# Weight conversion shared by ScalarE and VectorE, views for V's parts, and a scheduler that counts the port of VectorE and GpSimd

## The chip, the cores and the metric

One core of a Trainium2 chip runs one launch. The metric is the device time of that launch in microseconds (us), the median over runs. PE is TensorE's matmul stream and PEld its weight loads, DVE is VectorE, ACT ScalarE, POOL GpSimd, SP the queue that issues all DMAs.

## What is computed

Attention for 4 batches of 8 heads, sequence 576, head size 64, with scores below (row maximum - tau) cut off, then two gated layers of 512 x 1536:

```
scores = (q @ k.T) / 8
attn   = exp(where(scores >= max - tau, scores, -1e9) - max) / sum
x      = (attn @ v), heads side by side          # 2304 tokens x 512
xn     = x / sqrt(mean(x*x) + 1e-6) * rms_g
y      = (silu(xn @ w_gate) * (xn @ w_val)) @ w_out
out    = (silu(y @ w2_gate) * (y @ w2_val)) @ w2_out
```

The inputs q, k, v are float32. The six weight matrices arrive as float64, and the kernel makes them float32 on the chip.

## The kernel before

**Work units.** A batch of attention is 36 tiles of 128 queries (9 for each pair of heads, `tile_ops`). The two layers of a batch are 36 units (18 each): a unit is one slice of weights, 128 x 1024 elements, and 48 matmuls of 128x128 by 128x288. Every value that goes into a dense matmul stands there as two float32r parts, x0 = rounded x and x1 = x - x0, and three of the four products are taken (`dense`). A layer's `gate_val` unit makes one 128-row slice of the hidden values: tanh on ACT (L647), two products on DVE (L648, L659), a cast on ACT (L663) and the rest x - x0 on POOL or DVE (L666). `outp` units multiply those slices with the output weights and add up Y on DVE (L694).

**A tile** goes through QK on PE (L386), the negative row maximum on DVE (L409), the threshold and bias on DVE (L410, two elements), exp on ACT (L411), mask and sum on DVE (L412), small DVE operations and a reciprocal (L418 to L424), the normalisation (`normalise`, on ACT, DVE or POOL by a table), and a split into two float16 parts (`parts16`: a high part by a cast, L344 to L348; a low part in two subtractions, L352 and L353). DMA transposes (L358) bring the parts to PE, which multiplies them with V (`pv`, L444 and L447). `split` prepares V: two bfloat16 copies of the upper part (L304 or L306) and two subtractions (L311 or L313) for each head.

**Weights** (`weights(n)`, one call for each of the 36 units): load of 1 MB of float64 (L571), then five operations on the words: an absolute value of the upper word on ACT (L576), and on DVE a clamp (L579), a shift (L580) and two shift-and-or steps (L581, L582). Then a cast to float32r on ACT (L583), the rest on POOL (L584), and a store of both parts, 1 MB, to device memory (L585). Batches 1 to 3 load these stored parts (L565). The raw words have 2 buffers (`w64`), the float32 words 3 (`w32`), the split parts 3 (`w`).

**Order.** Nothing is ordered by hand. Each operation is put on record with an engine, a cost in ns, a priority and its dependences (`Program.op`). `Program.order` is a list scheduler: it always takes the engine that is free first and starts its ready operation of smallest priority, and the instructions are then issued in the order of the start times so found. Priorities are a due time, `SU(n)` for unit n and `ST(n)` for tile n, plus an offset from the tables `OFF` and, for the 36 tiles of batch 0, `OFFF`.

The attention of batch 0 runs alone. The dense units of batch 0 run beside the attention of batch 1 and the conversion of all weights, those of batches 1 and 2 beside the attention of batches 2 and 3, those of batch 3 alone.

Of the kernel before, what the change touches and what calls it, by code (L numbers as in the profile page):

```python
# [20 lines left out]
U64 = mybir.dt.uint64  # L21

# [52 lines left out]
class Program:  # L75


    def __init__(self):
        self.eng, self.cost, self.deps, self.fn, self.prio, self.lat, self.name, self.cols, self.rel = [], [], [], [], [], [], [], [], []
        self.wrote, self.read = {}, {}  # L80

    def op(self, eng, cost, fn, r=(), w=(), bufs=(), p=0.0, lat=None, name='', cols=None, rel=0.0):
# [21 lines left out]
        self.rel.append(rel)  # L104
        self.name.append(name)
# [3 lines left out]
    def order(self):  # L109
# [19 lines left out]
        out, seen = [], {}  # L129
        while len(out) < n:  # L130
# [10 lines left out]
            _, i = heapq.heappop(go[e])  # L141
            start[i] = t
# [36 lines left out]
def body(ctx: ExitStack, tc: tile.TileContext, qkv, tau, w1, rg, w2, outT):  # L179
# [19 lines left out]
    OFFF.update({'REC': -1394, 'PVO': 2852, 'THR': 2066, 'SQA': 9944, 'DT': -5666, 'PV': 13886, 'MAX': 1101, 'EXP': -137, 'MASK': 1731, 'LO': 3517, 'HI': -1687, 'SQ': -13503, 'NORM': 4425, 'LOL': -41192})
# [35 lines left out]
    r_raw = ring("raw", 4, [P, NQ], F32)  # L235
    r_v12 = ring("v12", 3, [P, 5, P], BF16)
# [12 lines left out]
    r_w64 = ring("w64", 2, [P, 1024], U64)  # L249
    r_w32 = ring("w32", 3, [P, 1024], F32)  # L250
# [551 lines left out]
```

## Time and profile before

| | |
|---|---|
| three runs | 1333.31, 1334.6, 1335.15 us, median 1334.6 |
| profiled execution | 1335.63 us, span 1333.8 us |
| busy over the span | PE 91%, PEld 80%, DVE 62%, ACT 44%, POOL 41% |
| granted TensorE clock, mean | 0.951 |
| DMA | 261.48 MB, mean 196 GB/s |

The profile shows one execution. Its span runs from the first to the last instruction; the execution's own time is 1.8 us longer. A share over the whole span mixes stages that differ, so it is read by stages. These are cut here at the first tanh of each batch's dense units (170, 527, 820 and 1105 us) and at the end of the last exp of batch 0 (125 us).

### The profile page before, as it was taken

Reading aid. Unit: us, or ns where it says so; the run is one execution under the profiler, and the core shown is the slowest. Engines: PE = TensorE matmul, PEld = TensorE weight load, DVE = VectorE, ACT = ScalarE, POOL = GpSimd, SP = SyncE. Lnnn points to the kernel's source line nnn. Section 1 sums busy time; section 2 is a strip of 40 time slices with the busy share of each in tenths; the row PEclk is TensorE's granted clock in tenths of the full one; section 3 lists DMA queues with packets and bytes.
Section 4 is the critical chain, followed back from the end, with each engine's and each line's share of the span. In section 5 each row is a group of like instructions: output and inputs, shape, how many; then the busy total and the mean of one; then the engine's idle time right before and its main releaser. Section 6 shows DMA issues by size and latency. Waiting matters only on the chain.

```text
span 1333.8 us, 21809 instructions
## 1 busy us (share of the span) xinstructions
PE 1211.9 (91%) x8528; PEld 1068.6 (80%) x8528; DVE 833.2 (62%) x1636; ACT 586.7 (44%) x878; POOL 545.7 (41%) x507
## 2 busy tenths in 40 slices
PE   4666669888889879999999999999999999999998
PEld 2334458777778778888888888888889899999998
DVE  6999798999999996545545565445554442122122
ACT  4555356645666544544444444544444321212111
POOL 4678566756666645323342423323431221012010
PEclk9767579999999889999999999999999999999999
DMA  7778748786888887976666658676556545454443
GB/s 219 158 183 195 216 140 251 218 253 188 255 245 238 243 271 205 286 211 186 186 188 185 181 161 229 186 192 195 175 164 170 164 169 181 164 177 166 158 168 122
DMA packets 204807, 261.48 MB, mean 196 GB/s; under 512 B 175008, under 2 KB 175648, under 8 KB 181664
## 3 DMA queue, kind: packets, MB, share of 16 engines
q1 hardware_dynamic: 204704, 260.08, 66.2%
q8 instruction: 67, 1.10, 0.3%
q14 instruction: 36, 0.29, 0.1%
HBM read 175.11 MB, written 42.47 MB: 163 GB/s over the span
## 4 chain that ended last, share of the span: by engine, by line
PE 63%; DVE 27%; issue 4%; ACT 3%; DMA 2%; POOL 1%; SPq 0%; DVEq 0%; ACTq 0%; POOLq 0%
PE ps L609 54%; PE ps L386 4%; DVE w L581 3%; DVE w L582 3%; PE pt L444 3%; DVE e L412 2%; DVE e L352 2%; DVE col L409 2%; DVE w L579 2%; DVE col L410 2%; PE pt L447 1%; DVE w L580 1%; DVE th L659 1%; DVE th L648 1%; DVE e L353 1%
## 5 line engine op out<-in xcount | busy, mean ns | idle before, releaser
L609 PE MATMUL ps<-XS,w 128*128 128x288 f32 x4608 | 661.7, 302 | 15.4 <-DVE th L648 4.4
L609 PEld LDWEIGHTS ps<-XS,w 128*128 128x128 f32 x4608 | 630.9, 192 | 55.2 <-issue 33.5
L609 PE MATMUL ps<-h,w 128*128 128x288 f32 x2304 | 322.1, 297 | 0.0
L609 PEld LDWEIGHTS ps<-h,w 128*128 128x128 f32 x2304 | 308.4, 189 | 17.1 <-issue 16.3
L666 POOL TENSOR_TENSOR h<-th,h 128x576 fp32r<-128x576 f32 x72 | 110.7, 1537 | 395.0 <-ACT h L663 386.6
L386 PE MATMUL ps<-raw 64*128 64x288 f32 (+1 forms) x640 | 121.7, 501 | 75.4 <-DVE e L412 49.9
L648 DVE SCALAR_TENSOR_TENSOR th<-th,ps 128x576 f32<-128x576 f32 x94 | 70.7, 752 | 184.2 <-ACT th L647 183.9
L411 ACT ACTIVATE e<-ps,col 128x576 f32<-128x576 f32 x126 | 93.3, 741 | 170.3 <-DVE col L410 164.4
L663 ACT CAST h<-th 128x576 fp32r<-128x576 f32 x96 | 64.7, 674 | 176.2 <-DVE th L659 175.9
L386 PEld LDWEIGHTS ps<-raw 64*128 64x128 f32 (+1 forms) x640 | 47.7, 195 | 113.4 <-DVE e L412 60.6
L409 DVE TENSOR_REDUCE col<-ps 128x1 f32<-128x576 f32 x144 | 107.7, 750 | 46.0 <-PE ps L386 45.3
L412 DVE SCALAR_TENSOR_TENSOR e<-ps,col,e 128x576 f32<-128x576 f32 x126 | 102.4, 813 | 48.1 <-ACT e L411 47.8
L333 ACT ACTIVATE e<-e,col 128x576 f32<-128x576 f32 x100 | 86.8, 868 | 81.0 <-DVE col L424 81.0
L584 POOL TENSOR_TENSOR w<-w,w 128x1024 fp32r<-128x1024 f32 x36 | 88.8, 2467 | 68.7 <-ACT w L583 63.7
L659 DVE SCALAR_TENSOR_TENSOR th<-th,ps 128x576 f32<-128x576 f32 x94 | 70.6, 751 | 68.8 <-PE ps L609 68.7
L444 PE MATMUL pt<-ag,v 128*128 128x256 f16 (+1 forms) x576 | 93.0, 313 | 19.7 <-DMA ag<-e 18.7
L647 ACT ACTIVATE th<-ps 128x576 f32<-128x576 f32 x94 | 61.1, 650 | 108.8 <-PE ps L609 108.1
L444 PEld LDWEIGHTS <-v 128*128 128x128 bf16 x576 | 55.7, 106 | 48.5 <-issue 14.2
L344 ACT CAST e<-e 128x576 f16<-128x576 f32 x122 | 81.7, 670 | 17.3 <-POOL e L329 13.3
L694 DVE TENSOR_TENSOR Y<-ps,Y 128x576 f32<-128x576 f32 x64 | 48.3, 755 | 64.0 <-PE ps L609 63.7
L352 POOL TENSOR_TENSOR e<-e,e 128x512 f16<-128x512 f32 x68 | 87.6, 1288 | 0.0
L353 POOL TENSOR_TENSOR e<-e,e 128x64 f16<-128x64 f32 x68 | 24.7, 364 | 105.6 <-ACT e L344 104.9
(89 smaller groups left out, 1061.8 us busy)
## 6 DMA issues: line engine op xcount, KB each, us to landing
w<-kept SPq DMA_DIRECT2D x108, 1024.0 KB, 4.9
w<-in_w SPq DMA_DIRECT2D x36, 1024.0 KB, 6.5
kept<-w SPq DMA_DIRECT2D x36, 1024.0 KB, 5.4
raw<-in_qkv SPq DMA_DIRECT2D x31, 736.0 KB, 5.2
out<-Y SPq DMA_DIRECT2D x16, 288.0 KB, 3.5
ag<-e SPq DMA_TRANSPOSE x160, 3.2
raw<-in_qkv SPq DMA_DIRECT2D x2, 160.0 KB, 2.8
raw<-in_qkv SPq DMA_DIRECT2D x1, 224.0 KB, 3.3
```

The source lines that it names most:

```text
L333: op("ACT", 765, lambda: nc.scalar.activation(e, e, AF.Identity, bias=c[:, 4:5], scale=c[:, 3:4]), **k)
L352: op(en, 610 if eng == 2 else 1113, lambda: n1.tensor_tensor(h[:, 640:], e[:, :512], h[:, :512], ALU.subtract), w=[("lo", n)], p=T + F['LO ...
L386: nc.tensor.matmul(s[m:m + w, j, :HS], x[k, c0:c0 + w], x[k, S + j * HS:S + (j + 1) * HS], start=True, stop=True)
L409: op("DVE", 668, lambda: nc.vector.tensor_reduce(c[:, 0:1], s2, AX.XY, ALU.max, negate=True), w=[sk, ("mx", n)], bufs=[cb], p=T + F['MAX'] ...
L411: op("ACT", 625, lambda: nc.scalar.activation(e2, s2, AF.Exp, bias=c[:, 2:3], scale=SCALE), r=[("thr", n)], w=[sk, ("e", n)] + ek, bufs=[c ...
L412: op("DVE", 730, lambda: nc.vector.scalar_tensor_tensor(e2, s2, c[:, 1:2], e2, ALU.is_ge, ALU.mult, accum_out=c[:, 6:7]), r=[("thr", n)], ...
L444: nc.tensor.matmul(pv_[:, :w], v12.t[:, i if i < 5 else i - 5, :], o[:, i, :w], start=(i == 0), stop=False)
L584: op("POOL", 2300, lambda: nc.gpsimd.tensor_tensor(ws[:, 1], w, f32(ws[:, 0]), ALU.subtract), r=[("w32", n), ("wh", n)], w=[("wl", n)], bu ...
L609: nc.tensor.matmul(pt[:, j, :HS], w(i, a), x(i, b_)[:, j * HS:(j + 1) * HS], start=(i == 0 and a == 0 and b_ == 0), stop=(i == n - 1 and a ...
L648: op("DVE", 670, lambda: nc.vector.scalar_tensor_tensor(t2, t2, 1.0, g2, ALU.add, ALU.mult), w=gk + [("th", n)], bufs=[tb], p=T + U + DRAI ...
L659: op("DVE", 670, lambda: nc.vector.scalar_tensor_tensor(t2, t2, 0.5, v2, ALU.mult, ALU.mult), w=vk + [("th", n)], bufs=[tb], p=T + 2 * U + ...
L666: op(eng, 670 if eng == "DVE" else 1360, lambda: n1.tensor_tensor(h[:, 1], tb.t, f32(h[:, 0]), ALU.subtract), r=[("th", n), ("h0", n)], w= ...
```

## The change

1. **Weights.** The 1 MB lands two bytes further in its buffer, so that the upper 16 bits of each float64 can be read as a bfloat16 and the 32 bits in the middle as an aligned word. Three ACT operations (two Prelu that scale and clamp, one Relu that shifts by 3 and adds the sign's place) make the upper 16 bits of the float32, negated. One DVE operation (L584) shifts the middle word by 13 and joins the two. Weights come out negated; the sign is taken back in the tanh scale of the first layer and in the last sum of Y. `w32` has 2 buffers instead of 3. Sixteen of the 36 rests (L588) go to DVE, by `W_E`.
2. **V.** V has a tile of its own, loaded by a DMA of its own (L305, 128 x 5 runs of 64 floats). Its upper part is the upper half of each float32, read through a view with a step of two; no copy is made. The two subtractions stay, on POOL or DVE by `V_E`.
3. **Threshold.** The constants of L412 (L410 before) are copied once into PSUM and read there.
4. **Scheduler.** Operations marked `lock`, and all of POOL, take turns in the planner's model (`port`). Costs, due times and offsets are new numbers.
5. **Tables of engines** (`NORM_E`, `HI_E`, `LO_E`, `H_E`, `X_E`, `P_E`) replace the old rules. For tiles of batch 0, 6 of 9 normalisations are on ACT instead of 2, none on DVE, and 3 of 9 low parts on DVE instead of 5. For batch 1 all normalisations are on ACT, 3 of 9 high parts on POOL, and 3 of 9 low parts on DVE instead of 4. Of the 24 rests of hidden slices (L671) of batch 0, 17 are on DVE instead of 6.

```diff
-        op("ACT", 950, lambda: nc.scalar.activation(w, t.bitcast(F32).rearrange("p (n t) -> p n t", t=2)[:, :, 1], AF.Abs),
-        op("DVE", 600, lambda: nc.vector.tensor_scalar(w, w, W_LO, W_HI, ALU.max, ALU.min), p=p + 1000, **k)
-        op("DVE", 600, lambda: nc.vector.tensor_scalar(u, u, 3, 0x3FFFFFF8, ALU.logical_shift_left, ALU.bitwise_and), p=p + 2000, **k)
-        op("DVE", 1135, lambda: nc.vector.scalar_tensor_tensor(u, lo, 29, u, ALU.logical_shift_right, ALU.bitwise_or), p=p + 3000, **k)
-        op("DVE", 1135, lambda: nc.vector.scalar_tensor_tensor(u, hi, 0xC0000000, u, ALU.bitwise_and, ALU.bitwise_or), p=p + 4000, **k)
+        op("DMA", 3000, lambda: nc.sync.dma_start(t[:, 1:4097], (w1, w2)[n // NU][n % NU].bitcast(U16)), ...
+        top = t.bitcast(BF16)[:, 4:4100:4]
+        mid = t.bitcast(U32)[:, 1:2049:2]
+        q, qi, qu = [bb.t.bitcast(d)[:, 1::2] for d in (BF16, I16, U16)]
+        op("ACT", 1100, lambda: nc.scalar.activation(q, top, AF.Prelu, scale=2.0 ** -56, alpha=2.0 ** 112), bufs=[b64, bb], p=p, **k)
+        op("ACT", 1100, lambda: nc.scalar.activation(q, q, AF.Prelu, scale=2.0 ** -56, alpha=2.0 ** 112), bufs=[bb], p=p + 1000, **k)
+        op("ACT", 1150, lambda: nc.scalar.activation(qu, qi, AF.Relu, scale=8.0, bias=half), bufs=[bb], p=p + 2000, **k)
+        op("DVE", 1200, lambda: nc.vector.scalar_tensor_tensor(w.bitcast(U32), mid, 13, bb.t, ALU.logical_shift_right, ALU.bitwise_or), lock=True,
...
-        vcopy(ea, V1, ("v1", hd), v12)
-        vsub(es, V, V1, [("v1", hd)], [v12])
-        vcopy(ea, V2, ("v2", hd), v12)
-        vsub(es, V3, V2, [("v2", hd), ("rawv", hd)], [v12, v3])
+        for i, (o, x, y, key, bs) in enumerate(((R, V, 0, ("v2", hd), [v]), (v3.t, R, 1, ("v3", hd), [v, v3]))):
+            eng = 2 * hd + i in V_E
...
-        op("DVE", 130, lambda: nc.vector.scalar_tensor_tensor(c[:, 1:3], K1, c[:, 0:1], K2, ALU.mult, ALU.add), ...
+        op("DVE", 200, lambda: nc.vector.scalar_tensor_tensor(c[:, 1:3], s[:, 1, KC:KC + 2], c[:, 0:1], K2, ALU.mult, ALU.add), ...
...
+            if self.lock[i]:
+                t = max(t, port)
+                port = t + self.cost[i]
```

**VectorE, in the middle of the first dense stage, before** (`w` the weight words, `th` a hidden slice, `col` a tile's small values, `ps` PSUM, `Y` the output sum):

```order
L579 TENSOR_SCALAR w_128<-w_128 128x1024
L648 SCALAR_TENSOR_TENSOR th_122<-th_122,ps_67 128x576
L424 RECIPROCAL col_106<-col_106 128x1
L409 TENSOR_REDUCE col_107<-ps_65 128x1
L580 TENSOR_SCALAR w_128<-w_128 128x1024
L410 SCALAR_TENSOR_TENSOR col_107<-K_79,col_107,K_80 128x2
L581 SCALAR_TENSOR_TENSOR w_128<-w_124,w_128 128x1024
L412 SCALAR_TENSOR_TENSOR e_102,col_107<-ps_65,col_107,e_102 128x576
L659 SCALAR_TENSOR_TENSOR th_122<-th_122,ps_66 128x576
L418 TENSOR_SCALAR col_107<-col_107 128x1
L419 TENSOR_SCALAR col_107<-col_107 128x1
L582 SCALAR_TENSOR_TENSOR w_128<-w_124,w_128 128x1024
```

**and in the changed kernel:**

```order
L584 SCALAR_TENSOR_TENSOR w_129<-w_127,t_131 128x1024
L700 SCALAR_TENSOR_TENSOR Y<-ps_66,Y 128x576
L414 SCALAR_TENSOR_TENSOR e_103,col_111<-ps_65,col_111,e_103 128x576
L420 TENSOR_SCALAR col_111<-col_111 128x1
L421 TENSOR_SCALAR col_111<-col_111 128x1
L411 TENSOR_REDUCE col_111<-ps_65 128x1
L426 RECIPROCAL col_111<-col_111 128x1
L412 SCALAR_TENSOR_TENSOR col_111<-ps_65,col_111,K_82 128x2
L653 SCALAR_TENSOR_TENSOR th_125<-th_125,ps_67 128x576
L664 SCALAR_TENSOR_TENSOR th_125<-th_125,ps_66 128x576
L414 SCALAR_TENSOR_TENSOR e_104,col_111<-ps_65,col_111,e_104 128x576
L584 SCALAR_TENSOR_TENSOR w_128<-w_126,t_130 128x1024
```

Four weight operations stood on DVE between two of a tile's steps; one stands there now, and the next unit's follows after two tiles' work.

**ScalarE, in the same stage, before:**

```order
L647 ACTIVATE th_122<-ps_67 128x576
L411 ACTIVATE e_102<-ps_65,col_109 128x576
L576 ACTIVATE w_126<-w_124 128x1024
L344 CAST e_105<-e_101 128x576
L333 ACTIVATE e_102<-e_102,col_109 128x576
L461 ACTIVATE pvt_115<-pt_68 64x320
L344 CAST e_103<-e_102 128x576
L463 ACTIVATE X_85<-pt_68 64x320
L583 CAST w_131<-w_128 128x1024
L411 ACTIVATE e_99<-ps_65,col_110 128x576
L663 CAST h_117<-th_122 128x576
```

**and in the changed kernel** (`t` the joined upper bits):

```order
L581 ACTIVATE t_130<-w_126 128x1024
L464 ACTIVATE pvt_117<-pt_68 64x320
L582 ACTIVATE t_130<-t_130 128x1024
L586 CAST w_134<-w_129 128x1024
L413 ACTIVATE e_101<-ps_65,col_112 128x576
L668 CAST h_119<-th_125 128x576
L652 ACTIVATE th_124<-ps_67 128x576
L583 ACTIVATE t_130<-t_130,half 128x1024
L466 ACTIVATE X_87<-pt_68 64x320
L335 ACTIVATE e_104<-e_104,col_112 128x576
L581 ACTIVATE t_131<-w_127 128x1024
```

A unit has four operations of 1024 columns on ACT instead of two, and the three of the conversion lie apart, with a tile's exp and a unit's tanh between them.

## Rows read from the trace of the kernel before

**Rows 1.** Busy time by stage: us, then PE, PEld, DVE, ACT, POOL, clock, DMA share, GB/s

```profile
0.00:125.00 125.00, 73.01 (x351) 35.02 (x352) 108.42 (x261) 66.83 (x106) 80.66 (x107) 0.78 0.79 189
125.00:170.00 45.00, 30.77 (x167) 25.40 (x166) 38.27 (x49) 18.23 (x28) 30.72 (x27) 0.67 0.67 193
170.00:527.00 357.00, 307.19 (x2092) 266.67 (x2091) 339.71 (x547) 203.57 (x285) 220.21 (x156) 0.94 0.77 230
527.00:820.00 293.00, 291.35 (x2135) 259.94 (x2135) 155.43 (x382) 136.41 (x212) 97.69 (x109) 1.00 0.71 200
820.00:1105.00 285.00, 284.63 (x2090) 256.93 (x2088) 137.71 (x330) 122.02 (x190) 86.44 (x91) 1.00 0.61 181
1105.00:1334.00 229.00, 224.91 (x1705) 224.67 (x1703) 53.63 (x71) 39.64 (x60) 29.94 (x21) 1.00 0.45 160
```

**Rows 2.** The same for instructions on weight words alone (tile w), first three stages

```profile
0.00:125.00 125.00, 1.45 (x9) 1.45 (x10) 10.29 (x10) 6.59 (x6) 4.71 (x2) 0.78 0.79 189
125.00:170.00 45.00, 18.83 (x101) 17.14 (x100) 21.40 (x15) 5.48 (x5) 4.69 (x2) 0.67 0.67 193
170.00:527.00 357.00, 248.39 (x1650) 232.95 (x1649) 159.61 (x119) 66.45 (x61) 79.43 (x32) 0.94 0.77 230
```

**Rows 3.** DVE by line, 170 to 527 us: busy us, mean ns, idle before

```profile
L582 DVE SCALAR_TENSOR_TENSOR w<-w,w 128x1024 uint32<-128x1024 uint32 x30 | 54.3, 1808 | 0.1
...
L410 DVE SCALAR_TENSOR_TENSOR col<-K,col,K 128x2 f32<-128x2 f32 x42 | 25.4, 604 | 0.3
L352 DVE TENSOR_TENSOR e<-e,e 128x512 f16<-128x512 f32 x19 | 21.8, 1146 | 0.0
...
L353 DVE TENSOR_TENSOR e<-e,e 128x64 f16<-128x64 f32 x19 | 9.3, 492 | 0.1
...
L666 DVE TENSOR_TENSOR h<-th,h 128x576 fp32r<-128x576 f32 x6 | 6.1, 1023 | 0.0
```

**Rows 4.** Four DVE lines over the whole span: ns min/median/max

```profile
L410 DVE SCALAR_TENSOR_TENSOR col<-K,col,K x144: 207/223/2385, 13.4 to 1057.3; 128x2 f32<-128x2 f32 x144
...
L582 DVE SCALAR_TENSOR_TENSOR w<-w,w x36: 1203/1225/5018, 78.7 to 505.4; 128x1024 uint32<-128x1024 uint32 x36
...
L352 DVE TENSOR_TENSOR e<-e,e x58: 676/684/2771, 46.5 to 1063.0; 128x512 f16<-128x512 f32 x58
...
L666 DVE TENSOR_TENSOR h<-th,h x24: 744/759/1810, 214.3 to 1318.7; 128x576 fp32r<-128x576 f32 x24
```

**Rows 5.** ACT by line, 170 to 527 us

```profile
L583 ACT CAST w<-w 128x1024 fp32r<-128x1024 f32 x32 | 33.5, 1046 | 14.3 <-DVE w L582 14.2
L576 ACT ACTIVATE w<-w 128x1024 f32<-128x1024 f32 x29 | 33.2, 1144 | 3.7 <-DMA w<-in_w 3.2 <-POOL w L584 0.4
L333 ACT ACTIVATE e<-e,col 128x576 f32<-128x576 f32 x37 | 32.1, 868 | 48.0 <-DVE col L424 48.0
...
L344 ACT CAST e<-e 128x576 f16<-128x576 f32 x42 | 28.1, 669 | 6.8 <-POOL e L329 6.1
```

**Rows 6.** DMA issues, 170 to 527 us: count, KB each, median us to landing

```profile
kept<-w SPq DMA_DIRECT2D x32, 1024.0 KB, 5.4
w<-in_w SPq DMA_DIRECT2D x28, 1024.0 KB, 6.5
...
ag<-e SPq DMA_TRANSPOSE x46, 3.2
```

**Rows 7.** Busy time in two single stretches, columns as in rows 1

```profile
450.00:500.00 50.00, 42.69 (x290) 37.86 (x289) 48.99 (x82) 25.86 (x35) 24.64 (x19) 0.93 0.93 285
1150.00:1320.00 170.00, 170.00 (x1290) 170.00 (x1289) 42.29 (x56) 29.79 (x45) 24.23 (x17) 1.00 0.46 162
```

**Rows 8.** The waits, 125 to 170 us: us in total, times, longest

```profile
PE pt L444 <- DMA ag<-e: 11.1, 2, 6.2
```

**Rows 9.** Weight loads into PE over the whole span: ns min/median/max

```profile
L444 PEld LDWEIGHTS <-v x576: 95/98/152, 25.4 to 1068.4; 128*128 128x128 bf16 x192
```

```profile
L609 PEld LDWEIGHTS ps<-XS,w x4608: 186/188/338, 123.5 to 1316.7; 128*128 128x128 f32 x192
```

More of the change, by code (lines that the diff above doesn't have):

```diff
@@ L128, in order @@
                 arrive(i)
-        out, seen = [], {}
+        out, seen, port = [], {}, 0.0
         while len(out) < n:
@@ L393, in tile_ops @@
                 r += [("rawk", 0, 0), ("rawk", 0, 1), ("rawq", 0, 0), ("rawq", 0, 1)]
-        op("PE", 490 * len(parts), QK, r=r, w=[sk], bufs=[raw[hd] for hd, *_ in parts], p=T, name=f"QK{n}")
+        op("PE", 690 * len(parts), QK, r=r, w=[sk], bufs=[raw[hd] for hd, *_ in parts], p=T, name=f"QK{n}")
         if not second:
@@ L422, in tile_ops @@
         if whole or second:
[L423 to L424 removed]
+            op("DVE", 240, smalls, lock=True, r=[("sum", i) for i in two], w=[("rec", i) for i in two], bufs=[cb], p=T + F['REC'], name=f"REC{n}")
+            op("DVE", 150, lambda: nc.vector.reciprocal(cc(3), cc(5)), w=[("rec", i) for i in two], bufs=[cb], p=T + F['REC'], name=f"RECI{n}")
             for i in two:
@@ L460, in pv @@
         sk = ("SS", gr)
-        op("ACT", 53 + w * 83 // 100, lambda: nc.scalar.activation(tmp, pv_[r:r + 64, :w], AF.Copy, scale=1.0 / UPP), w=[vk, ("pvt", n)], bufs=[tb], p=T + F['PVO'], name=f"PVout{n}")
-        if not last and g % NP in (0, 1, 2):
-            op("ACT", 53 + w * 83 // 100, lambda: nc.scalar.activation(x, pv_[m0:m0 + 64, :w], AF.Copy, scale=1.0 / UPP), w=[vk, xk], bufs=[], p=T + F['PVO'], name=f"PVout{n}")
-            op("POOL", 149 + w * 21 // 10, lambda: nc.gpsimd.tensor_tensor(x, x, tmp, ALU.add), r=[("pvt", n)], w=[xk], bufs=[tb], p=T + F['PVA'], name=f"PVout{n}")
+        op("ACT", 150 + w * 83 // 100, lambda: nc.scalar.activation(tmp, pv_[r:r + 64, :w], AF.Copy, scale=1.0 / UPP), w=[vk, ("pvt", n)], bufs=[tb], p=T + F['PVO'], name=f"PVout{n}")
@@ L465, in pv @@
+        if not last and 4 * g + gr not in X_E:
+            op("ACT", 150 + w * 83 // 100, lambda: nc.scalar.activation(x, pv_[m0:m0 + 64, :w], AF.Copy, scale=1.0 / UPP), w=[vk, xk], bufs=[], p=T + F['PVO'], name=f"PVout{n}")
+            op("POOL", 250 + w * 21 // 10, lambda: nc.gpsimd.tensor_tensor(x, x, tmp, ALU.add), r=[("pvt", n)], w=[xk], bufs=[tb], p=T + F['PVA'], name=f"PVout{n}")
         else:
-            op("DVE", 75 + w * 105 // 100, lambda: nc.vector.scalar_tensor_tensor(x, pv_[m0:m0 + 64, :w], 1.0 / UPP, tmp, ALU.mult, ALU.add), r=[("pvt", n)], w=[vk, xk], bufs=[tb], p=T + F['PVO'], name=f"PVout{n}")
+            op("DVE", 140 + w * 105 // 100, lambda: nc.vector.scalar_tensor_tensor(x, pv_[m0:m0 + 64, :w], 1.0 / UPP, tmp, ALU.mult, ALU.add), r=[("pvt", n)], w=[vk, xk], bufs=[tb], p=T + F['PVO'], name=f"PVout{n}")
@@ L532, in norm @@
         for c in range(NC):
-            put(c, X2[b % 2][:, c], [("Xn", b, c)] + [("X", b % 2, c, g) for g in range(4)], [], T, ("DVE", "POOL")[(1, 1, 1, 1)[c]])
+            put(c, X2[b % 2][:, c], [("Xn", b, c)] + [("X", b % 2, c, g) for g in range(4)], [], T, ("POOL", "DVE")[8 * b + c in P_E])
     NRAW = 2
```

208 lines of the change are left out of this document (102 added, 106 removed).

## The prediction

> **What bounds the kernel now.** I read the busy times by stage first, since a share over the span mixes stages with different limits [rows 1]. In the last two stages (820 to 1105 and 1105 to 1334 us) PE is busy without a gap at clock 1.00 and every other engine has time to spare: 285 us for 36 units beside attention, 229 us for 36 units alone. The second dense stage takes 293 us, 8 more than the third for the same work. The first takes 357 us. There DVE is busy 339.7 us, 95%, while PE has 50 us of gaps, a clock of 0.94, and ACT is used for 57%. The instructions on weight words show why: 159.6 us of DVE's time there are the conversion [rows 2]. So the first dense stage is bound by DVE, and without that bound PE's 285 us would be next. Before it, the attention of batch 0 takes 125 us with DVE at 87% and DMA at 79%, and a tail of 45 us follows, in which DVE is busy 38.3 us, 21.4 of them with weights [rows 1, 2].
>
> The second thing to see is that DVE's time there is partly waiting inside instructions. The shift-and-or has a median of 1225 ns and a mean of 1808 in this stage; the threshold step of two elements has 223 and 604, with single ones of 2385; the low part 684 and 1146 [rows 3, 4]. All of them have two SBUF operands, and POOL is busy 62% of this stage [rows 1]. The masks and maxima from PSUM aren't among these lines.
>
> **First dense stage, engine by engine.**
>
> DVE: 339.7 - 159.6 (the four conversion steps) + 31 joins + 13 weight rests + 11 hidden rests - threshold - low parts + V. The join is a shift-and-or of the same size: 1.23 us clean, 1.81 as met in this stage; I take 1.5, since POOL loses work too: 46 us. The weight rests have no DVE row; bounded by the same 1.23 and 1.81, I take 1.4: 18. Hidden rests 0.76 to 1.02: 10. Threshold: 42 x (604 - 223 ns) = 16 off, if one PSUM operand ends the wait; 0 if not. Six low parts fewer: 6 x (1146 + 492 ns) = 10 off. About 11 V subtractions, each at most a hidden rest: 8. Sum 236 us, and 265 with every upper price [rows 1 to 4]. Either way below PE's 285.
>
> ACT: 203.6 - 33 (the absolute values) + 31 units x 3 operations + 5 normalisations x 0.87 - 11 casts x 0.67. For the new three the nearest rows are the absolute value, which also reads every second word (1.14 us), and the contiguous cast (1.05). The 16-bit operands with a step aren't in the trace; I take 1.14 to 1.2, 109 us in all. Sum 277 us [rows 1, 5]. That is close to PE's 285, so ACT's order matters: the 48 us that normalisations waited for DVE's reciprocal are gaps that must close [rows 5].
>
> *A rule against it.* ACT's row shows 1.14 us for 1024 columns, DVE's clean shift-and-or 1.23, so an element costs the two engines about the same here [rows 4, 5]. The Trainium skill, "ScalarE: Activation LUTs", section Rules for kernel authors, says relu, max, min, add and mul belong on VectorE, not ScalarE. By that rule the move would lose time, as rival 2 works out; the rows say that ACT has time to spare and DVE hasn't.
>
> DMA: now 0.77 x 357 = 275 us. A 1 MB transfer takes 2.9 us of it: in the last stage 27 units (1290 matmuls, 48 each) cost 0.46 x 170 = 78 us [rows 7]. By the instruction order 25 loads and 25 stores stood between batch 1's first and batch 2's first transpose, now 28 and 29; so up to 7 transfers, 20 us, move in. 285 to 295 us. Two unknowns here: a destination two bytes off (0, or the 1.1 us by which a float64 load lands later than a store of the same size [rows 6], 40 us over 36 loads) and V's load as 256-byte runs. I take 0 for both, since bytes and row lengths of the loads stay. The Trainium skill, "DMA: Bandwidth & Descriptors", section How a descriptor splits into AXI transactions, says that a transfer off a 256-byte start costs one more transaction, an estimate of 33 for 32 here, 3 us for all loads; no row of this trace shows an unaligned transfer.
>
> So four resources stand at 285 (PE), 285 to 295 (DMA), 277 (ACT) and 236 (DVE). How near a stage gets to its bound: DVE reached 95% over 357 us, and DMA 93% over the busiest 50 us [rows 1, 7]. 285 / 0.95 = 300; 285 / 0.93 = 306 and 295 / 0.93 = 317. I take 308 us, bounds 288 (PE alone) and 340 (DMA at 85%): 49 us gained.
>
> **Front.** DVE 108.4, less 10.3 for weights [rows 2], 36 x 0.2 for the threshold, 7 low parts at 0.9 to 1.6 and 4 normalisations: about 80 us. ACT 66.8 + 15 normalisations and 4 casts: about 81. POOL stays near 70. DMA is now the largest: 0.79 x 125 = 98 us, some 95 after, at 0.93 102 us. I take 105, bounds 102 and 125. What is late next is the transposes: three buffers for the 16-bit parts, 3.2 us to landing [rows 6].
>
> **Tail.** 45 us, of which DVE's 21.4 on weights become some 5 joins and one rest, 7.5 us. The other part is a chain: the last transposes (PE waited 11.1 us for them [rows 8]), V products, the sum of squares, the scale. I take 31, the 14 us of DVE that leave; bounds 24, what DVE still has to do, and 45.
>
> **Costed at nothing.** The view of V steps by two in PE's weight load: 98 ns now, 188 for four-byte elements [rows 9]; but the dense stream loads at 188 and still runs at 170 / 1290 = 132 ns a matmul [rows 7], so the load hides behind the stream. Without that cover it would be 90 ns for each of 896 loads, 81 us. V's two copies for each head go from POOL and ACT; off the path. The second dense stage loses some 5 of its 8 extra us, left over from DVE's backlog. The last two stages are PE alone and stay.
>
> **Sum.** 105 + 31 + 308 + 288 + 285 + 229 = 1246 us, against 1334 by the same cuts. The execution's own time was 1.8 us over its span and 1.0 over the median: 1247 us for the median.
>
> **Rivals.**
> 1. *DMA holds the first dense stage at 340.* For it: 0.93 in the busiest stretch, landings of 6.5 us there. Against: DVE's wait was never for a load; ACT's was 3.2 us [rows 5]. 1279 us.
> 2. *ACT becomes the bound:* 16-bit operands with steps at 1.8 us instead of 1.14 make 31 x 5.4 = 167, 335 us in all; at 0.95, 353. Against: a cast to 16 bits takes 0.67 us for 576 columns, in line with 1.05 for 1024 to 32 bits [rows 5]. 1292 us. That is how the rule quoted above from the Trainium skill would come out here.
> 3. *Both floors are met:* front 102, tail 26, first dense stage 288, second 285. 1216 us.
> 4. *Slower: the two buffers of raw words.* A buffer is taken for the load, three ACT steps with other work between them, and the join. 6.5 + 3.4 + about 3.5 (the five operations between them in the order) + 1.2 = 14.6 us, plus waits in DVE's queue; two units may take 17.1 at 308 us. If a round takes 22.0 us (18 rounds, 396 us), nothing is gained, and at 23 the time is 1353. Before, two units took 19.8 us. Against: that needs 7 us of waits that now have no cause on a freed DVE.
> 5. *It doesn't do what it says:* the freed DVE time is filled by port waits, since joins and rests also have two SBUF operands. At the prices as met DVE has 265 us, still not the bound. Only if PE's gaps had another cause would the time stay at 1335.
>
> **Chances.** Forecast (first dense stage 295 to 325) 0.55, rival 1 0.22, rival 2 0.05, rival 3 0.11, rival 4 0.05, rival 5 0.02. The range goes from rival 3, 1216, to a front of 110, a tail of 40 and 340 after them, 1295. Faster by over 0.2% (2.7 us, about what a measurement of this kernel can tell) 0.93, within it 0.02, slower 0.05.
>
> **What would show it.** Right: the first dense stage at about 308 us with DVE below 85%, ACT near 90%, DMA over 0.9, clock near 1.00; last two stages at 285 and 229; threshold steps with a mean near 223 ns. Wrong: the three ACT operations far from 1.14 us; ACT waiting for loads (lines of the conversion behind a DMA) by more than some 30 us; PE's weight loads of V above 100 ns with a longer third dense stage; a tail still at 45 us, which would mean that its chain and not DVE set it.

## The result and the profile after

The changed kernel takes 1260.8 us (median of 4 runs, 1255.5 to 1262.7) against 1334.9 (4 runs): 0.944 of the time before, 95% interval 0.941 to 0.947. 74 us are gained where 88 were forecast. The profiled execution is the run of 1255.5 us, its span 1253.7. Two runs in this study were slow, one of the kernel before (1389.5 us, granted clock 0.82) and one of four of the kernel without the port rule (6366 us), and no number below uses them.

The same stages (last exp of batch 0, first tanh of each batch's dense units) are now cut at 104, 146, 445, 737 and 1023 us. Busy time of the changed kernel by stage, columns as in [rows 1]:

```profile
0.00:104.00 104.00, 61.81 (x328) 29.91 (x328) 84.72 (x236) 76.87 (x120) 60.83 (x87) 0.85 0.82 189
104.00:146.00 42.00, 30.72 (x169) 24.36 (x170) 26.24 (x43) 35.91 (x44) 21.41 (x18) 0.76 1.00 297
146.00:445.00 299.00, 288.86 (x2097) 254.19 (x2096) 232.53 (x462) 265.48 (x325) 142.47 (x118) 1.00 0.94 275
445.00:737.00 292.00, 292.00 (x2136) 260.32 (x2135) 179.13 (x442) 107.28 (x171) 72.58 (x83) 1.00 0.77 199
737.00:1023.00 286.00, 286.00 (x2102) 257.54 (x2101) 157.00 (x387) 99.95 (x160) 77.14 (x81) 1.00 0.67 182
1023.00:1254.00 231.00, 226.82 (x1705) 226.36 (x1703) 59.69 (x79) 39.67 (x60) 18.58 (x13) 1.00 0.45 159
```

| stage | before | forecast | after |
|---|---|---|---|
| front | 125 | 105 | 104 |
| tail | 45 | 31 | 42 |
| first dense | 357 | 308 | 299 |
| second | 293 | 288 | 292 |
| third | 285 | 285 | 286 |
| last | 229 | 229 | 231 |

In the first dense stage PE has 10 us of gaps instead of 50 and its clock is 1.00 instead of 0.94; DVE is down from 95% to 78%, ACT up from 57% to 89%, DMA from 77% to 94%. The lines of DVE and ACT in that stage (146 to 445 us), to set beside [rows 3, 5]:

```profile
L584 DVE SCALAR_TENSOR_TENSOR w<-w,t 128x1024 uint32<-128x1024 uint32 x30 | 40.2, 1342 | 10.0 <-ACT t L583 6.4 <-issue 2.6 <-POOL v L320 0.9
L671 DVE TENSOR_TENSOR h<-th,h 128x576 fp32r<-128x576 f32 x17 | 23.0, 1354 | 6.2 <-ACT h L668 6.2
L588 DVE TENSOR_TENSOR w<-w,w 128x1024 fp32r<-128x1024 f32 x15 | 20.2, 1346 | 1.3 <-ACT w L586 1.1
L354 DVE TENSOR_TENSOR e<-e,e 128x512 f16<-128x512 f32 x13 | 8.9, 683 | 0.0
L412 DVE SCALAR_TENSOR_TENSOR col<-ps,col,K 128x2 f32<-128x2 f32 x39 | 8.5, 218 | 0.1
```

```profile
L583 ACT ACTIVATE t<-t,half 128x1024 uint16<-128x1024 int16 x29 | 42.3, 1458 | 0.1
L581 ACT ACTIVATE t<-w 128x1024 bf16<-128x1024 bf16 x29 | 40.2, 1385 | 4.8 <-DMA w<-in_w 4.8
L582 ACT ACTIVATE t<-t 128x1024 bf16<-128x1024 bf16 x29 | 39.7, 1370 | 0.2
L586 ACT CAST w<-w 128x1024 fp32r<-128x1024 f32 x32 | 33.2, 1037 | 2.3 <-DVE w L584 2.3
L335 ACT ACTIVATE e<-e,col 128x576 f32<-128x576 f32 x36 | 30.7, 854 | 1.0 <-DVE col L426 0.9
```

The clamp, the shift and the two shift-and-or steps are gone, and one join at a mean of 1342 ns stands for them. The threshold's mean fell from 604 to 218 ns. Normalisations on ACT had waited 48 us for the reciprocal and now wait 1. The three new ACT operations take 1.37 to 1.46 us each.

The chain of waits of the same stage, by line, before and after:

```profile
by line: DVE w L582 11.9%; issue 11.8%; DVE w L581 10.5%; PE ps L609 7.7%; DVE e L412 6.8%; DVE w L579 5.9%; DVE col L409 5.6%; DVE e L352 5.2%; DVE col L410 4.8%; DVE th L659 4.0%; DVE th L648 3.9%; DVE w L580 3.8%; DVE e L353 2.1%; DVE Y 
```

```profile
by line: PE ps L614 61.2%; PE ps L388 6.9%; PE pt L447 5.4%; issue 3.9%; PE pt L450 2.3%; ACT t L581 2.1%; ACT t L582 1.8%; ACT w L586 1.7%; ACT t L583 1.6%; DVE w L584 1.5%; ACT e L413 1.3%; ACT XS L547 1.1%; ACT e L335 0.8%; ACT th L652 0
```

The conversion on DVE led that chain (32% for its four lines); now PE's dense matmuls do (61%). The weight loads of V through the view, to set beside [rows 9]:

```profile
L447 PEld LDWEIGHTS <-v x576: 96/98/152, 23.9 to 999.2; 128*128 128x128 bf16 x192
```

### The profile page after: what moved, and what is told of

Read it like the earlier page. It is cut to its first block, busy times and chain, and to the rows that moved or that the text cites. A ratio compares the mean times of both kernels' runs of the same rounds, so it can differ in the third digit from the quotient of the medians.

```text
span 1253.7 us, 21723 instructions
## 1 busy us (share of the span) xinstructions
PE 1186.2 (95%) x8528; PEld 1052.7 (84%) x8528; DVE 739.3 (59%) x1643; ACT 625.2 (50%) x875; POOL 393.0 (31%) x399
## 3 DMA queue, kind: packets, MB, share of 16 engines
q1 hardware_dynamic: 225552, 260.09, 73.6%
## 4 chain that ended last, share of the span: by engine, by line
PE 83%; ACT 5%; DVE 3%; issue 1%; DMA 1%; POOL 0%; ACTq 0%; DVEq 0%; POOLq 0%
PE ps L614 71%; PE ps L388 5%; PE pt L447 4%; PE pt L450 2%; ACT t L581 1%; ACT t L583 1%; ACT t L582 1%; DVE w L584 1%; DMA ag<-e 1%; ACT w L586 0%; PE ps L518 0%; ACT e L346 0%; ACT e L413 0%; DVE e L414 0%; ACT e L335 0%
## 5 line engine op out<-in xcount | busy, mean ns | idle before, releaser
L614 PEld LDWEIGHTS ps<-XS,w 128*128 128x128 f32 x4608 | 619.9, 189 | 44.3 <-issue 30.8
L614 PE MATMUL ps<-XS,w 128*128 128x288 f32 x4608 | 648.5, 299 | 7.6 <-ACT XS L542 2.3
L671 POOL TENSOR_TENSOR h<-th,h 128x576 fp32r<-128x576 f32 x45 | 65.7, 1459 | 298.4 <-ACT h L668 298.4
L388 PE MATMUL ps<-raw 64*128 64x288 f32 (+1 forms) x640 | 115.1, 480 | 34.8 <-DVE Y L414 16.4
L447 PE MATMUL pt<-ag,v 128*128 128x256 f16 (+1 forms) x576 | 89.7, 306 | 15.9 <-DMA ag<-e 9.6
L354 POOL TENSOR_TENSOR e<-e,e 128x512 f16<-128x512 f32 x68 | 80.8, 1188 | 0.0
L355 POOL TENSOR_TENSOR e<-e,e 128x64 f16<-128x64 f32 x68 | 27.0, 397 | 160.1 <-ACT e L346 111.5
L700 DVE SCALAR_TENSOR_TENSOR Y<-ps,Y 128x576 f32<-128x576 f32 x64 | 48.2, 755 | 46.5 <-PE ps L614 45.6
L346 ACT CAST e<-e 128x576 f16<-128x576 f32 x88 | 58.6, 666 | 27.1 <-POOL e L331 15.1
L335 ACT ACTIVATE e<-e,col 128x576 f32<-128x576 f32 x72 | 61.8, 858 | 13.4 <-DVE col L426 13.2
L588 POOL TENSOR_TENSOR w<-w,w 128x1024 fp32r<-128x1024 f32 x20 | 48.3, 2415 | 55.7 <-ACT w L586 45.1
```

The costliest lines, as they stand in the source:

```text
L335: op("ACT", 865, lambda: nc.scalar.activation(e, e, AF.Identity, bias=c[:, 4:5], scale=c[:, 3:4]), **k)
L354: op(en, 670 if eng == 2 else 1170, lambda: n1.tensor_tensor(h[:, 640:], e[:, :512], h[:, :512], ALU.subtract), lock=True, w=[("lo", n)], ...
L388: nc.tensor.matmul(s[m:m + w, j, :HS], x[k, c0:c0 + w], x[k, S + j * HS:S + (j + 1) * HS], start=True, stop=True)
L447: nc.tensor.matmul(pv_[:, :w], v12[:, i if i < 5 else i - 5], o[:, i, :w], start=(i == 0), stop=False)
L614: nc.tensor.matmul(pt[:, j, :HS], w(i, a), x(i, b_)[:, j * HS:(j + 1) * HS], start=(i == 0 and a == 0 and b_ == 0), stop=(i == n - 1 and a ...
L671: op(eng, 720 if eng == "DVE" else 1430, lambda: n1.tensor_tensor(h[:, 1], tb.t, f32(h[:, 0]), ALU.subtract), lock=True, r=[("th", n), ("h ...
```

## Experiments

Times are medians; a ratio is the time over that of the kernel before, with its 95% interval. "Stages" are the lengths of front, tail, first dense, second, third and last in us, cut as above from each run's profile (a row's own cut can lie up to 1 us off). The theory (A): DVE's conversion bound the first dense stage and PE bounds it now. The main rivals: the tables and the planner brought the gain; ACT or DMA is the new bound. For the tail: ACT's queue, the DMA queue, or the steps of the last tiles themselves.

### The conversion alone, in the kernel before

```diff
-        op("DVE", 1135, lambda: nc.vector.scalar_tensor_tensor(u, lo, 29, u, ALU.logical_shift_right, ALU.bitwise_or), p=p + 3000, **k)
...
+        op("ACT", 1100, lambda: nc.scalar.activation(q, top, AF.Prelu, scale=2.0 ** -56, alpha=2.0 ** 112), bufs=[b64, bb], p=p, **k)
...
+        op("DVE", 1200, lambda: nc.vector.scalar_tensor_tensor(w.bitcast(U32), mid, 13, bb.t, ALU.logical_shift_right, ALU.bitwise_or),
```

> The kernel before with only the new conversion of weights (part 1, with its sign changes and buffers); tables, planner, V and threshold stay as before. Theory A (DVE's conversion was the bound of the first dense stage): that stage falls from 357 us to 300-325 us, DVE's share there below 85%, the whole to 1270-1300 us. Rival B (the tables of engines and due times bring the gain): the stage stays over 345 us and the whole over 1320 us.

1291.6 us, ratio 0.969 (0.967 to 0.970). Stages 124, 36, 316, 294, 287, 231.

```profile
124.00:160.00 36.00, 29.50 (x189) 23.84 (x188) 21.78 (x37) 27.78 (x38) 25.20 (x26) 0.86 0.68 207
160.00:476.00 316.00, 295.11 (x2088) 257.37 (x2087) 232.00 (x458) 276.63 (x340) 197.12 (x153) 0.97 0.89 263
```

Part 1 by itself gains 42.5 us. By the profile the first dense stage gives 41 and the tail 10, the front didn't move, and the last three stages take back 5. DVE is at 73% in the first dense stage. That is what theory A expects and rival B does not.

### All but the conversion

```diff
-        op("ACT", 1100, lambda: nc.scalar.activation(q, top, AF.Prelu, scale=2.0 ** -56, alpha=2.0 ** 112), bufs=[b64, bb], p=p, **k)
...
+        op("ACT", 1100, lambda: nc.scalar.activation(w, t.bitcast(F32).rearrange("p (n t) -> p n t", t=2)[:, :, 1], AF.Abs),
+        op("DVE", 670, lambda: nc.vector.tensor_scalar(w, w, W_LO, W_HI, ALU.max, ALU.min), p=p + 1000, **k)
...
```

> The changed kernel with the old conversion (one ACT and four DVE operations, three w32 buffers, positive signs); views of V, threshold, planner and tables stay as changed. Theory A: the first dense stage goes from 299 us back to 340-365 us, DVE at 93% or more there, the whole 1305-1335 us. Rival B: the whole stays below 1275 us.

1323.9 us, ratio 0.993 (0.991 to 0.995). Stages 104, 64, 347, 292, 286, 229.

```profile
104.00:168.00 64.00, 40.45 (x212) 33.06 (x213) 58.92 (x73) 28.77 (x42) 33.94 (x21) 0.67 0.74 238
168.00:515.00 347.00, 300.58 (x2060) 261.51 (x2059) 310.20 (x544) 186.05 (x258) 149.14 (x115) 0.95 0.80 236
```

Parts 2 to 5 alone give 10 us. The front is as short as in the full change, but 19 of the 21 us come back in the tail, where DVE is busy 92%. Conversions that the longer front used to hold now stand there; on weight words alone the engines have in these two stages (DVE is the third pair)

```profile
0.00:104.00 104.00, 0.00 (x0) 0.00 (x0) 0.00 (x0) 2.24 (x2) 0.00 (x0) 0.79 0.81 184
104.00:168.00 64.00, 23.79 (x118) 21.87 (x119) 38.30 (x33) 12.07 (x11) 8.97 (x3) 0.67 0.74 238
```

so DVE has no weight work in the front and 38 us in the tail, against 10 and 21 before [rows 2]. In the first dense stage DVE is at 89%, not at the 93% I expected, so its work alone doesn't fill that stage; that the rest is order is argued, not shown. Of the whole gain (about 75 us), 42 are part 1 alone, 10 the rest alone, and 22 exist only with both. By the profiles some 12 of those 22 lie in the tail, where the shorter front pays only when DVE has no backlog behind it, 8 in the first dense stage and 3 after it.

### Less work on ACT, on DMA, on both

The first cuts the three ACT operations to 64 of 1024 columns, the second the float64 loads to 256 of 4096 16-bit columns, from unit 2 on; the third does both. The planned order stays, and these kernels leave out most of the weights' values.

```diff
+        cn = 64 if n >= 2 else 1024
-        op("ACT", 1100, lambda: nc.scalar.activation(q, top, AF.Prelu, scale=2.0 ** -56, alpha=2.0 ** 112), bufs=[b64, bb], p=p, **k)
+        op("ACT", 1100, lambda: nc.scalar.activation(q[:, :cn], top[:, :cn], AF.Prelu, scale=2.0 ** -56, alpha=2.0 ** 112), bufs=[b64, bb], p=p, **k)
...
+        cl = 256 if n >= 2 else 4096
-        op("DMA", 3000, lambda: nc.sync.dma_start(t[:, 1:4097], (w1, w2)[n // NU][n % NU].bitcast(U16)), ...
+        op("DMA", 3000, lambda: nc.sync.dma_start(t[:, 1:1 + cl], (w1, w2)[n // NU][n % NU].bitcast(U16)[:, :cl]), ...
```

> The changed kernel in the same order, with the three ACT operations of the conversion on 64 of 1024 columns from unit 2 on, so most of the weights' upper halves are left out; ACT loses about 130 us of work, nothing else changes. If PE is what sets the first dense stage now, it stays within 5 us of 299 us and the tail of 42 us alone falls, by 5-10 us, because three conversion operations stand ahead of the attention's there: whole 5-15 us less. If ACT sets the stage, it falls to 286-290 us: whole 15-25 us less. If neither, under 4 us less.

> The changed kernel in the same order, with the loads of float64 weights from unit 2 on cut to 256 of 4096 16-bit columns, so those units compute with words left over in the buffer; 34 MB leave the DMA queue. DMA's share of the first dense stage falls from 0.94 to about 0.65. If the transposes behind the weight loads set the tail, it falls from 42 us to 32-36 us. If DMA sets the first dense stage (rival 1 of the prediction), that falls from 299 to 286-291 us. If PE and ACT set them, the whole is less than 5 us shorter.

> The changed kernel in the same order, with both cuts at once: the ACT operations of the conversion on 64 columns and the loads of float64 weights on 256, from unit 2 on. If the tail is held by two chains of about the same length (ACT's queue, and loads ahead of the transposes), it falls from 42 us by more than the two single cuts gave together (2 us), to 34-38 us. If it is held by neither, but by the steps of the last tiles, PE's own work and the sum of squares in their order, it stays at 39-42 us. The first dense stage: 288-294 us in either case, since PE's 288 us of work stay.

ACT cut: 1250.5 us; loads cut: 1255.1; both: 1248.7. The changed kernel, measured again:

> The changed kernel itself once more, as the measure for the others of this group: 1255-1263 us, stages of 104, 42, 298, 292, 286 and 230 us in its profile.

1258.7 us (1257.0 to 1259.5), stages 107, 42, 298, 292, 286, 231; the measure for the runs around it. Tail and first dense stage with ACT cut, with the loads cut, and with both:

```profile
106.00:146.00 40.00, 31.22 (x176) 24.30 (x176) 25.68 (x42) 21.08 (x45) 23.66 (x18) 0.74 1.00 308
146.00:440.00 294.00, 288.41 (x2086) 254.80 (x2087) 228.94 (x462) 178.16 (x324) 145.82 (x118) 0.99 0.95 281
```

```profile
104.00:146.00 42.00, 31.04 (x169) 24.65 (x170) 27.35 (x43) 35.80 (x44) 23.39 (x18) 0.76 0.56 159
146.00:444.00 298.00, 289.05 (x2092) 255.10 (x2092) 232.38 (x461) 264.70 (x324) 142.41 (x118) 0.99 0.63 184
```

```profile
104.00:144.00 40.00, 30.83 (x176) 24.13 (x176) 26.60 (x43) 21.36 (x46) 24.63 (x18) 0.74 0.59 169
144.00:438.00 294.00, 288.31 (x2086) 254.70 (x2087) 228.88 (x462) 177.92 (x324) 145.05 (x118) 0.99 0.64 187
```

DMA at 0.63 instead of 0.94 leaves both stages as they were: rival 1 is out, a share of 0.94 hid nothing here. The median is 3.6 us lower; between the two profiles the difference lies in the front (104 us against 107), which differs by that much between profiles of one order. ACT without its 87 us gives 4 to 5 us in the first dense stage and 2 in the tail; PE's 288 to 289 us of work fill what is left. So PE bounds the first dense stage, and ACT adds some 5 us of gaps. (PE's own work was not cut; DVE is the engine left, at 78%, and 9 us more on it made the stage 2 us longer in the run with the constants in SBUF below.) The tail is held by neither queue: with both cut it still takes 39 us. My forecast of 5 to 10 us from ACT in the tail is a miss. I had read that price from the changed kernel's chain of 100 to 150 us:

```profile
by line: DMA ag<-e 13.6%; issue 11.3%; ACT t L583 8.4%; DVE w L584 7.6%; ACT t L581 7.0%; DVE tok L510 5.4%; ACT t L582 5.2%; PE ps L518 4.8%; ACT XS L547 4.2%; POOL e L355 3.1%; DVE e L414 3.1%; ACT e L346 2.7%; ACT pvt L471 2.5%; POOL e L
```

The conversion's three ACT lines have 21% of it, 10 us, and were worth 2 when cut: other work stood nearly as long, as the chain in the next section shows. Even the 2 us may not be ACT's. In the changed kernel PE waited 2.5 us in the tail for one DVE operation on five columns (L510), which took 2.33 us instead of its median of 0.17; with ACT cut, alone or with the loads, it took 0.17 and that wait was gone. The two causes weren't separated.

### The last low parts on DVE

With both cut, POOL's low parts (L354, L355) led the chain of 100 to 148 us:

```profile
by line: POOL e L354 10.5%; PE ps L616 8.0%; DVE X L527 7.0%; DMA ag<-e 6.8%; POOL e L355 5.8%; POOL w L590 5.0%; PE pt L447 4.3%; PE pt L495 4.0%; POOL XS L549 4.0%; ACT w L588 3.8%; issue 3.6%; DVE w L586 3.6%; ACT XS L542 3.3%; POOL SS L
```

```diff
+        if 32 <= n < NFAST:
+            n1 = nc.vector
```

> The changed kernel, planned in the same order, but the low parts of the last four tiles of batch 0 are issued on DVE in place of POOL (three tiles change, six subtractions). With both cuts of the run before, the chain of the tail went through POOL's low parts for some 8 of 48 us and DVE was idle for 14 of 42 us. If those subtractions are what the last transposes wait for, the tail falls from 42 us to 37-40 us and the whole by 2-5 us. If DVE's queue delays them as much (joins that wait for ACT stand in it), the whole stays within 2 us of 1259 us.

1257.9 us, ratio 0.942 (0.940 to 0.944): no difference. Its tail is 41 us, where 37 to 40 was expected of a tail that POOL's low parts held. A miss. That several chains of like length end together there fits all four runs and is argued, not shown.

### The threshold's constants, and the two bytes

```diff
-        op("DVE", 200, lambda: nc.vector.scalar_tensor_tensor(c[:, 1:3], s[:, 1, KC:KC + 2], c[:, 0:1], K2, ALU.mult, ALU.add), ...
+        op("DVE", 200, lambda: nc.vector.scalar_tensor_tensor(c[:, 1:3], K0, c[:, 0:1], K2, ALU.mult, ALU.add), ...
```

> The changed kernel with the threshold's constants read from SBUF instead of PSUM (part 3 undone), same order. The threshold's mean in the first dense stage should go from 218 ns back to 400-600 ns, 8-16 us more of DVE there. If DVE is no longer the bound, the whole is less than 3 us longer; if DVE's order still sets PE's gaps, 5-15 us longer. The front, where DVE is busy over 80%, may lose 2-5 us.

1261.7 us, 0.945 (0.943 to 0.947): 3 us above the changed kernel, with intervals that overlap. The threshold in the first dense stage:

```profile
L412 DVE SCALAR_TENSOR_TENSOR col<-K,col,K 128x2 f32<-128x2 f32 x39 | 17.1, 438 | 0.1
```

One operand in PSUM ends the wait (a mean of 218 ns against 438 here, the longest of 144 at 224 ns against 1729), but that is worth 9 us of an engine that no longer bounds the stage, and the 3 us of time aren't clear of the spread.

```diff
-        op("DMA", 3000, lambda: nc.sync.dma_start(t[:, 1:4097], (w1, w2)[n // NU][n % NU].bitcast(U16)), ...
+        op("DMA", 3000, lambda: nc.sync.dma_start(t[:, 0:4096], (w1, w2)[n // NU][n % NU].bitcast(U16)), ...
...
-        mid = t.bitcast(U32)[:, 1:2049:2]
+        mid = t.bitcast(U32)[:, 0:2048:2]
```

> The changed kernel with the float64 weights loaded to the start of the buffer instead of two bytes further, same order and same sizes; the words are then read at wrong places, so the weights are wrong. If a destination two bytes off costs DMA time, the packets per load and the DMA share of the first dense stage (0.94) fall, to about 0.8 by the upper price of the prediction (1.1 us a load), and loads land about 1 us earlier. If it costs nothing, both stay. The time should not change by more than 3 us, since taking the loads away gave less than that in the first dense stage.

1258.1 us; the words are read at wrong places, so the weights are wrong. Packets of the changed kernel, whole span:

```profile
DMA packets 225656, 261.48 MB, mean 209 GB/s; under 512 B 195985, under 2 KB 196497, under 8 KB 202513
...
q1 hardware_dynamic: 225552, 260.09, 73.6%
```

of this run:

```profile
DMA packets 225655, 261.48 MB, mean 208 GB/s; under 512 B 195984, under 2 KB 196496, under 8 KB 202512
...
q1 hardware_dynamic: 225552, 260.09, 73.2%
```

and of the changed kernel measured again:

```profile
q1 hardware_dynamic: 225552, 260.09, 73.0%
```

No cost of the offset shows. The queue's packets are the same, its share without the offset lies between the two profiles with it, and loads in the first dense stage land after 6.7 us instead of 6.8. The DMA work did grow against the kernel before, from 66.2% of 1333.8 us (883 us) to 73.6% of 1253.7 (923), with the same bytes and 20,849 more packets. The runs of 256 bytes in which V is now loaded are 32 x 128 x 5 = 20,480. V's loads weren't tried alone, but two runs above narrow it down: part 1 alone, with all 36 offset loads and V as before, has 68.4% of 1288.5 us (881 us); parts 2 to 5, with V's new loads and no offset, have 69.0% of 1322.6 (913 us). So some 30 of the 40 us come with parts 2 to 5, and none with part 1 alone.

### The tables of batch 0, and the port in the planner

```diff
-NORM_E = [(2, 2, 1, 2, 2, 1, 1, 2, 0), (1, 1, 1, 1, 1, 1, 1, 1, 1), (1, 1, 0, 1, 0, 1, 0, 1, 1)]
+NORM_E = [(2, 2, 1, 2, 2, 1, 1, 2, 0), (1, 1, 1, 1, 1, 1, 1, 1, 1), (2, 1, 0, 0, 0, 0, 0, 0, 1)]
-LO_E = [(2, 0, 0, 0, 2, 2, 0, 2, 2), (0, 0, 0, 0, 0, 2, 2, 0, 2), (2, 0, 0, 2, 0, 0, 0, 2, 0)]
+LO_E = [(2, 0, 0, 0, 2, 2, 0, 2, 2), (0, 0, 0, 0, 0, 2, 2, 0, 2), (2, 0, 2, 0, 2, 0, 2, 0, 2)]
...
```

> The changed kernel with the old tables for the tiles of batch 0 (normalisations 1 of 9 on DVE, 2 on ACT, 6 on POOL; low parts 5 of 9 on DVE; high parts as before). If the prediction's account of the front holds (DVE from 108 to 80 us by low parts and normalisations given away, DMA then the largest), the front goes from 104 us to 115-126 us, and the stages after the tail stay at 298, 292, 286 and 230 us. If due times and costs made the front short, it stays at 103-109 us.

1282.7 us, 0.961 (0.959 to 0.963). Stages 123, 48, 300, 292, 286, 231. The first 122 us:

```profile
0.00:122.00 122.00, 69.31 (x331) 33.65 (x332) 92.43 (x256) 69.67 (x106) 64.51 (x91) 0.78 0.78 179
```

With the old tables the front is 15 to 19 us longer than in the profiles of the changed kernel's order, and the tail some 6 longer. So the short front needs the new tables. That is the time which the prediction's account gave, but not its reason: DVE is busy only 76% of this front, so its work doesn't fill it. The due times were chosen for the new tables, and the run can't tell what the assignment costs by itself from what it costs with due times that don't fit it.

```diff
-        self.lock.append(lock or eng == 'POOL')
+        self.lock.append(False)
```

> The changed kernel with the planner's turns for the port taken out (part 4's rule undone: operations marked lock no longer wait for one another in its model); costs, due times and tables stay, so the order differs. If the rule matters, the order no longer fits the chip: front and tail lose 5-15 us and the whole goes to 1265-1285 us. If the port's waits are hidden behind PE anyway, the whole stays within 4 us of 1259 us.

1263.2 us (three runs), 0.947 (0.945 to 0.948): 4 to 5 us more than the changed kernel, between the two expectations. Its first dense stage takes 303 us instead of 298; front and tail, where I had looked for the loss, take 147 together against 149. The costs and due times were chosen with the rule in place, so this compares two orders; what the rule is worth with numbers chosen without it is not shown.

### A version planned anew

```diff
-        op("ACT", 1100, lambda: nc.scalar.activation(q, top, AF.Prelu, scale=2.0 ** -56, alpha=2.0 ** 112), bufs=[b64, bb], p=p, **k)
+        op("ACT", 1250, lambda: nc.scalar.activation(q, top, AF.Prelu, scale=2.0 ** -56, alpha=2.0 ** 112), bufs=[b64, bb], p=p, **k)
...
-UP, FP, T0, DRAIN, ATT, LEAD, UL, RMS0, RMS1, CREL = 6528, 2381, 131281, -3653, 5021, 6, 5309, 47142, -24070, 49597
+UP, FP, T0, DRAIN, ATT, LEAD, UL, RMS0, RMS1, CREL = 6484, 2741, 139304, -14154, 4963, 6, 4729, -3992, -67763, 50428
...
```

> The changed kernel with the planner's costs of the three ACT operations of the conversion set from 1100, 1100 and 1150 ns to 1250, 1250 and 1320 (what they take in a row on the chip) and of the products with V to 14 matmuls instead of 12, and with engine tables, due times and offsets chosen anew so that the planner's own last time is least. If the too low costs are what holds the front, the tail and the first dense stage above PE's floor, the three together fall from 444 us to 432-440 us and the whole to 1243-1254 us. If the tail is a chain of steps that no order shortens and the first dense stage is PE's 289 us, the whole stays within 3 us of 1259 us.

1257.3 us, 0.941 (0.940 to 0.943): not to be told from the changed kernel. Front, tail and first dense stage of its profile, which is of its longest run (1264.5 us):

```profile
0.00:97.00 97.00, 56.85 (x316) 28.77 (x317) 76.78 (x218) 70.59 (x110) 64.11 (x96) 0.83 0.86 192
97.00:149.00 52.00, 35.77 (x199) 28.05 (x197) 36.07 (x59) 41.92 (x53) 22.76 (x19) 0.76 0.90 261
149.00:454.00 305.00, 293.08 (x2090) 256.48 (x2091) 224.56 (x456) 256.36 (x309) 158.51 (x132) 0.98 0.94 274
```

The three together take 454 us, not the 432 to 440 that the first expectation asked for. Front and tail take 149 us, as in every kernel of this study with the new conversion and the new tables (144 to 151), wherever the cut between them falls. What holds that sum is not settled.

## Why the prediction was right, and where it was not

**The bound.** Right. DVE held the first dense stage; without the conversion's four steps it has 232.5 us of work there (forecast 236) and PE's chain leads. The stage came out at 299 us, 9 under the forecast: PE reached 97% of it (288.9 of 299), where I had taken the 93 to 95% that DVE and DMA had shown in the kernel before. Those shares belonged to other engines; of PE's 10 us of gaps the cut of ACT took 4 to 5. That DVE's work met its forecast is partly luck: the hidden rests added 17 us instead of 10, since they waited (1354 ns each, clean 748), and the low parts fell by 19 instead of 10. The upper sum that I gave as 265 us is some 270 by its own prices, and the range's upper end 1293; neither changes the argument. One reading was too narrow: the waits inside DVE's instructions weren't only in those with two SBUF operands. The clamp and the shift with one (L579, L580 before) had medians of 694 and 688 ns over the span and means of 971 and 1001 in that stage.

**The front.** Right in number (104 against 105), not in its reason. DMA was to be its bound with some 95 us and is busy 0.82 x 104 = 85 us; DVE is busy 84.7 us (forecast 80), ACT 76.9 and POOL 60.8. None of them fills the stage, so what bounds it is open, and that the sum met it is in part luck.

**ACT's price.** Mis-sized: 1.37 to 1.46 us an operation instead of 1.14 to 1.2, 122 us for the three instead of 109. The total of ACT was still under the forecast (265 against 277). The other work came to 143 us instead of 168. Half of that the trace shows: the durations of ACT's operations in that stage sum to 292 us, so 27 us of them lie over one another, against 13 before. The rest is mostly attention's operations: 17 fewer casts instead of 11, and one normalisation less where I had added five. Rival 2's condition (1.8 us) was not met, and neither was its consequence. The Trainium skill, "ScalarE: Activation LUTs", section Rules for kernel authors, puts max, min, add, mul and relu on VectorE. The traces agree for the single operation, though on other operands: 1.37 to 1.46 us for each of the three on ACT, and a median of 0.69 us for the clamp (max and min) that DVE had before. They don't agree for the move: the run with part 1 alone gained 42.5 us.

**DMA.** 0.94 x 299 = 281 us, just under 285 to 295. The load two bytes off costs nothing, as taken. The Trainium skill, "DMA: Bandwidth & Descriptors", section How a descriptor splits into AXI transactions, says that a descriptor which doesn't start on a 256-byte boundary begins with a transaction from the boundary below; for rows of 8192 bytes that makes 33 instead of 32, an estimate of 3 us over all loads. The page words it for reads, and here it is the written side that is off. No run here shows it: the share without the offset (73.2%) lies between two profiles with it (73.0% and 73.6%). V's loads were costed at nothing because "bytes and row lengths of the loads stay". That sentence was wrong for V: 20,849 packets were added. No time of the first dense stage went with it, since the run with the loads cut shows DMA to have slack there; what it costs in the front wasn't tried.

**The tail.** "I take 31, the 14 us of DVE that leave": the step that failed, by 11 us. DVE did fall (26 us of 42 busy), and with the old tables 10 of the 14 us did leave (36 us in the run with part 1 alone). With the new tables the front ends 20 us sooner, and work that it held went to the tail. The transfers of weights in the changed kernel's tail:

```profile
w<-in_w SPq DMA_DIRECT2D x6, 1024.0 KB, 7.0
kept<-w SPq DMA_DIRECT2D x4, 1024.0 KB, 7.2
```

and in the tail of part 1 alone:

```profile
w<-in_w SPq DMA_DIRECT2D x2, 1024.0 KB, 6.5
kept<-w SPq DMA_DIRECT2D x2, 1024.0 KB, 4.6
```

with five joins in the first and one in the second. I kept before's content of the tail and only subtracted from it. At 42 us it is near the 45 that I had named as a sign that its chain and not DVE sets it. That this work is what keeps the tail at 42 us is not shown: without ACT's share of it or the loads it still takes 39, the four runs on the tail found no single cause, and it stays open. A forecast for front and tail together (136 us) would have missed 146 by 10 just the same. The first dense stage came out 9 us under its forecast, so the two misses nearly cancel in the sum, which is luck.

**The rest.** The second stage kept 6 us over the third, of which I had expected 5 to go (288 against 292). It isn't "the same work": PE is busy without a gap in both, with 2136 matmuls against 2102 (20 more of QK, 14 more with V), and rows 1 had 2135 against 2090. So this is PE's own work and not DVE's backlog. The stages sum to 1254 against 1246. Another 5 us of the 14 between forecast and median lie between the profiled run and the median. Eight profiles of the same planned order show where such a spread can lie: the front took 104.0 to 108.1 us in them, the first dense stage of the five that cut no work 298.3 to 300.1.

**Costed at nothing.** V's view: 98 ns a load as before, right. The wait in the threshold, which the forecast took off DVE's sum: right in size (604 to 218 ns), small in time. Rival 4, the two raw buffers: no sign; ACT waited 4.8 us for loads.

## What to carry to other kernels

When an engine's work is taken off a stage that it bound, size the stage by the next engine's own work, and check the next bound by cutting work in a fixed order: here a queue at 94% had slack, and 21% of a chain was worth 2 us. Before subtracting from a stage, ask what a planner will move into it across the cut. A short front paid here only without a backlog behind it: 10 us and 42 us alone made about 75 together.

## What the runs showed of the hardware

The three ACT operations on 1024 16-bit columns with a step (of two; the first reads with a step of four) took 1.37 to 1.46 us, where a cast of as many contiguous words took 1.04 and the old absolute value on every second 32-bit word 1.14 [rows 5]; whether type, step or function costs it wasn't separated. A DMA that lands two bytes off the start of a row had the same number of packets and the same median landing time to 0.1 us. The waits inside DVE's instructions have not gone from the changed kernel but moved: hidden rests on DVE have a median of 759 ns over the span and a mean of 1354 in the first dense stage, and an operation of five columns met one of 2331:

```profile
L671 DVE TENSOR_TENSOR h<-th,h x51: 748/759/2562, 162.1 to 1238.7; 128x576 fp32r<-128x576 f32 x51
```

```profile
L510 DVE SCALAR_TENSOR_TENSOR tok<-tok,tok x12: 165/166/2331, 135.0 to 1008.5; 128x5 f32<-128x5 f32 x12
```

The start and end times tell what they wait for. All ten hidden rests that took over 900 ns ended 603 to 620 ns after the end of a POOL operation that ran beside them, and the long one of five columns 19 ns after one. So did the 43 of 144 threshold steps before that took over 300 ns (5 to 26 ns after), and the 13 of 36 clamps over 800 ns (547 to 574 ns after). In these operations DVE seems to start its own work only when POOL's operation is over; with one operand in PSUM none of 144 threshold steps took more than 224 ns.
